# A new order of all engines for a two-block kernel (polynomial-sketch attention, then an MLP), with the products of VectorE and GpSimd kept apart

## The chip, the cores and the metric

The kernel runs on one core of one Trainium2 chip. The metric is the time of one execution in device microseconds (us). The engines are named as in the profile: PE is TensorE, PEld its weight loads, DVE VectorE, ACT ScalarE, POOL GpSimd, SP SyncE.

## The reference

All inputs are float32 except where the kernel decodes 64-bit words (the sketch matrices S1 and S2 and the two MLP weights are handed over as raw 64-bit floats and turned into float32 on the chip).

```python
# attention: batch 4, heads H=4, S=1088 tokens, D=32, r=8
def phi(x):                      # 64 features per token and head
    a = einsum('rd,bhsd->bhsr', S1, x); b = einsum('rd,bhsd->bhsr', S2, x)
    return einsum('bhsi,bhsj->bhsij', a, b).reshape(..., r*r)
q_p, k_p = phi(q), phi(k)
kv  = einsum('bhsf,bhsd->bhfd', k_p, v);  z = sum(k_p, axis=2)
num = einsum('bhsf,bhfd->bhsd', q_p, kv)
den = einsum('bhsf,bhf->bhs', q_p, z)[..., None] + 1e-06
x = (num / den) as (B, S, H*D)             # rows of 128
# MLP block, 128 -> 512 -> 128
xn = (x - mean) / sqrt(var + 1e-06) * g_ln
out = x + maximum(xn @ w_ch1, 0) @ w_ch2
```

## The kernel before, in words

The kernel is one long list of small operations, written as a string, `PROGRAM`, of 518 entries. Each entry names a Python function, which issues one to a few dozen instructions, and gives its arguments: the engine (V = DVE, A = ACT, G = POOL, S = the SP queue), the batch b or chunk c, the range u0 to u1 of the nine token groups of a batch, and banks of PSUM. No scheduler reorders anything afterwards: each engine executes its own entries in the order of the list, and waits only where data or a buffer demands it. An engine that has nothing to wait for therefore runs ahead of the place at which its entry stands in the list.

For each batch b the work goes like this. `turn_g`, `turn_r` transpose q and k (DVE, lines 414 and 424). `k_dir` or `k_feat`, `q_dir` or `q_feat` project them (PE, lines 448, 466, 554 and 587), and `k_cp`, `k_tok`, `q_cp`, `q_tok` bring the projections back to SBUF as `kf` and `fq`. `k_prod` forms the 64 products per token and head, `kp` (line 87, `times`), except that `k_prod0` does it from PSUM; `k_val` multiplies them with v (PE, line 519), and `k_vcp`, `k_spr`, `k_rcp` lay the result out as `kvr`. On the side of q, `q_ac` (product), `q_den` (sum), `q_rec` (reciprocal), `q_a2` (product) make the divided features, `q_prod` the 64 products, `qp`, and `q_turn` transposes these to `qpT` (DVE, line 634). `num b` (PE, line 648) then makes the rows of the attention; `num_cp` copies them to `xT` for the MLP, and `row_turn`, `row_wr`, `row_rd` bring the same rows, by way of DRAM, into `x` for the mean, variance and residual.

The MLP goes by chunks c of four groups of 128 rows (two chunks a batch; chunks 8 and 9 hold the ninth groups). `hid` is the first layer (PE, line 757), `relu` its activation (ACT or DVE), `sec` the second layer (PE, line 773). `st_bn`, `st_ag`, `st_pow` make 1/sqrt(var) (the power on POOL, line 743); `fin` (DVE) or `fin_a` with `fin_g` (ACT, then DVE or POOL, line 801) scale and add the residual, and `store` writes the result.

Before batch 0 the weights are decoded: `w_ex`, `w_bits`, `w_exf`, `w_mant`, `w_low`, `w_e2`, `w_e3`, `w_add`, `w_mul` (w = 0 for S1 and S2, 1 and 2 for the MLP's weights). `w_e3` (line 310) and `w_add` (line 315) have two operands in SBUF, as has `times`. `c_cg` and `fold` work the mean and the gain into the first weight. `fill` (line 247) is a product of ones with ones into a bank that nobody reads.

```python
    def times(eng, o, a, b):
        by[eng].tensor_tensor(out=o, in0=a, in1=b, op=ALU.mult)
    ...
    for line in PROGRAM.split(";"):
        if line.split():
            name, *args = line.split()
            ops[name](*(int(a) if a.isdigit() else a for a in args))
```

## Time and profile before

| | us |
|---|---|
| time, median of 3 runs (lowest, highest) | 107.59 (107.14, 107.84) |
| time of the profiled execution | 107.5 |
| its span in the profile | 105.6 |
| PE busy | 98.7 (93%) |
| DVE busy | 84.4 (80%) |
| POOL busy | 49.4 (47%) |
| ACT busy | 37.3 (35%) |

The span is what the trace covers; about 1.9 us of the profiled execution's time lie around it. The granted clock of TensorE was 1.0 throughout. PE's busy time contains 13.3 us of `fill`. In a timeline, a row gives start and length of a piece, the engine, the line, what it writes and reads, the shape and how often; a note in brackets tells how long the engine was idle before it and who ended that.

### The profile page before, as it was taken

To read this page: it belongs to the slowest core of one execution; us is meant where nothing else is said; L and a number is where in the kernel's file an instruction comes from. 1 tells how busy PE (TensorE), PEld (TensorE's weight loads), DVE (VectorE), ACT (ScalarE), POOL (GpSimd) and SP (SyncE) were. 2 spreads that over 40 slices of the span, in tenths; PEclk is the share of its full clock that TensorE was granted. 3 is DMA by queue.
4 is the path that set the end of the run, shared out by engine and by line. 5 is a ranking of instruction groups with operands and counts; after the bars stand their busy time and mean duration, and the time that the engine had idled before them with its cause. 6 is when DMAs were issued, how large, how long until landed. Compare 5 with 4: busy or idle time off the path is not lost.

```text
span 105.6 us, 3155 instructions
## 1 busy us (share of the span) xinstructions
PE 98.7 (93%) x1276; PEld 69.7 (66%) x1276; DVE 84.4 (80%) x243; ACT 37.3 (35%) x91; POOL 49.4 (47%) x65
## 2 busy tenths in 40 slices
...
GB/s 72 295 261 238 221 395 271 18 9 57 221 286 292 335 263 110 0 6 112 156 238 10 6 6 6 167 70 262 112 0 6 8 210 286 8 99 105 99 75 50
DMA packets 12639, 14.37 MB, mean 136 GB/s; under 512 B 2128, under 2 KB 9296, under 8 KB 12624
## 3 DMA queue, kind: packets, MB, share of 16 engines
...
q14 instruction: 5, 0.04, 0.1%
...
## 4 chain that ended last, share of the span: by engine, by line
PE 68%; DVE 23%; issue 2%; POOL 2%; ACT 0%; DVEq 0%
PE ALL L757 26%; PE ALL L773 25%; PE ALL L648 5%; DVE qp L87 5%; PE ALL L247 5%; DVE qpT L634 3%; PE ALL L519 2%; PE ALL L587 2%; DVE kp L87 2%; DVE kf L475 1%; DVE fq L596 1%; DVE bits L310 1%; POOL ex L305 1%; DVE kT L414 1%; DVE st L730 1%
## 5 line engine op out<-in xcount | busy, mean ns | idle before, releaser
L773 PEld LDWEIGHTS ALL<-w,hT 128*128 128x128 f32 x272 | 32.3, 192 | 5.5 <-issue 3.1
L773 PE MATMUL ALL<-w,hT 128*128 128x128 f32 x272 | 33.8, 278 | 0.0
L757 PE MATMUL ALL<-xT,w 128*128 128x512 f32 (+1 forms) x72 | 30.3, 550 | 0.0
L765 ACT ACTIVATE hT<-ALL 128x512 f32<-128x512 f32 (+2 forms) x34 | 16.6, 518 | 23.5 <-PE ALL L757 23.1
L743 POOL TENSOR_TENSOR rstd<-va,mhalf 128x4 f32<-128x4 f32 (+1 forms) x10 | 9.7, 972 | 24.1 <-DVE va L737 21.7
L757 PEld LDWEIGHTS ALL<-xT,w 128*128 128x128 f32 x72 | 12.5, 191 | 7.3 <-issue 5.5
L87 POOL TENSOR_TENSOR kp<-kf 128x1280 f32<-128x1280 f32 (+2 forms) x7 | 14.6, 2089 | 3.5 <-DVE kf L475 3.5
L247 PE MATMUL ALL<-ones 128*128 128x256 f32 (+1 forms) x28 | 13.3, 594 | 1.4 <-DVE m L195 1.4
L634 DVE STREAM_TRANSPOSE qpT<-qp 128x1280 f32<-128x1280 f32 (+2 forms) x9 | 11.0, 1230 | 0.1
L87 DVE TENSOR_TENSOR qp<-a,fq 128x512 f32<-128x512 f32 (+2 forms) x6 | 9.8, 1640 | 0.0
L87 POOL TENSOR_TENSOR qp<-a,fq 128x512 f32<-128x512 f32 (+3 forms) x4 | 8.6, 2142 | 1.6 <-DVE a L87 1.4
L767 DVE TENSOR_SCALAR hT<-ALL 128x512 f32<-128x512 f32 (+2 forms) x10 | 4.9, 498 | 5.2 <-PE ALL L757 5.2
L648 PE MATMUL ALL<-qpT,kvr 32*32 32x288 f32 (+2 forms) x320 | 7.2, 364 | 1.7 <-ACT ob L791 1.3
L791 ACT ACTIVATE ob<-ALL,rstd 128x128 f32<-128x128 f32 x20 | 6.6, 376 | 6.3 <-POOL rstd L743 4.5
L82 ACT COPY xT<-ALL 128x256 f32<-128x256 f32 x10 | 6.2, 639 | 6.3 <-DVE xh L710 3.3
L247 PEld LDWEIGHTS ALL<-ones 128*128 128x128 f32 x28 | 5.5, 220 | 4.3 <-issue 2.5
L710 DVE STREAM_TRANSPOSE xh<-ALL 128x256 f32<-128x256 f32 x16 | 6.6, 425 | 1.2 <-PE ALL L648 1.0
L648 PEld LDWEIGHTS ALL<-qpT,kvr 32*32 32x32 f32 x320 | 4.1, 103 | 4.5 <-ACT ob L791 1.5
L786 DVE SCALAR_TENSOR_TENSOR ob<-ALL,rstd,x 128x128 f32<-128x128 f32 x12 | 4.0, 349 | 3.8 <-PE ALL L773 2.5
L730 DVE BATCH_NORM_STATS2 st<-x 128x6 f32<-128x128 f32 x32 | 6.7, 274 | 0.0
L596 DVE STREAM_TRANSPOSE fq<-ALL 128x576 f32<-128x576 f32 x6 | 4.4, 765 | 1.8 <-PE ALL L587 1.8
L519 PEld LDWEIGHTS ALL<-kp,vn 128*32 128x32 f32 x288 | 4.2, 110 | 1.4 <-issue 0.9
(113 smaller groups left out, 114.8 us busy)
## 6 DMA issues: line engine op xcount, KB each, us to landing
...
xd<-xh SPq DMA_DIRECT2D x8, 256.0 KB, 2.1
x<-xd SPq DMA_DIRECT2D x8, 256.0 KB, 3.5
out_dram<-ob SPq DMA_DIRECT2D x7, 256.0 KB, 2.4
...
w_raw<-in_moe_w_ch_dram SPq DMA_DIRECT2D x2, 256.0 KB, 5.0
```

The costliest lines, as they stand in the source:

```text
L87: by[eng].tensor_tensor(out=o, in0=a, in1=b, op=ALU.mult)
L247: pe.matmul(bank(z, 0, w), ones[:, 0:P], ones[:, 0:w], start=True, stop=True)
L519: pe.matmul(bank(z, 0, F)[D * h : D * h + D], vn[b][:, TW * h + D * u : TW * h + D * (u + 1)], kp[:, H * F * u + F * h : H * F * u + F * ( ...
L634: dve.transpose(_ap(qpT, 0, P, 32 * u0, [[32, u1 - u0], [TW, 8], [1, 32]]), qp[:, H * F * u0 : H * F * u1])
L648: pe.matmul(bank(z[r], o, o + w)[D * h : D * h + D], kvr[b % 2][rows, DM * f + D * h : DM * f + D * h + D], qpT[rows, c : c + w], start=(f ...
L710: dve.transpose(_ap(xh[slot(c)], 0, P, 64 * n * i, [[32 * n, 2], [32, n], [1, 32]]), pair(z, P * (c % 2), [[32, n], [1, 32]]))
L730: dve.bn_stats(out=sts[slot(c)][:, 6 * t : 6 * t + 6], in_=row_ap(c, t))
L743: pool.tensor_tensor(out=rstds[slot(c)][:, 0:n], in0=vas[slot(c)][:, 0:n], in1=mhalf[:, 0:n], op=ALU.pow)
L757: pe.matmul(bank(z, 0, n), w1[:, P * j : P * (j + 1)], cols(c)[:, a : a + n], start=True, stop=True)
L765: act.activation(o, i, AF.Relu)
L773: pe.matmul(bank(z, DM * t, DM * (t + 1)), h[:, 512 * j + P * t : 512 * j + P * (t + 1)], w2[:, DM * j : DM * (j + 1)], start=(j == 0), st ...
L791: act.activation(ob(c)[:, P * t : P * (t + 1)], bank(z, P * t, P * (t + 1)), AF.Copy, scale=rstds[slot(c)][:, t : t + 1])
```

## The change

Only the list is changed; every function is as before. The 518 entries become 517: one `fill` of 512 columns is left out. All others stay, in another order on all engines, with other banks of PSUM, and some on another engine. Those that change engine are:

- `w_exf 1 256 512`, `w_mant 1 256 512` from DVE to ACT; `w_mant 2`, `w_add 2` to DVE (from ACT and POOL); `w_e2 2` from DVE to POOL
- `k_cp` of groups 0 to 3 of batch 0, and `k_vcp 2`, from ACT to DVE; `k_rcp 3` and `row_cp 8` from DVE to ACT; two stores change queue between SP and ACT
- `q_ac 1` (swapped halves), `q_ac 2` to DVE and `q_ac 3` to POOL; `q_a2` of `1 0 4`, `2 0 4` and `3 4 9` from DVE to POOL
- `q_prod 2 4 9` and `q_prod 3 0 4` from DVE to POOL
- `fin_g 0` and `fin_g 1` from DVE to POOL; four copies `num_cp` net from DVE to ACT, four `relu` net from ACT to DVE

Two lines of the diff stand for the rest:

```diff
-    w_e3 V 1 0 256; q_cp A 0 4 7 0 24; fill 1 512 4; fill 1 256 7; q_cp A 4 9 3 0 24;
-    q_ac V 0 0 4; c_cg G; sk_8 6; q_den 0 0 4; w_mul G 1 0 256; ld S q 1 0 34; q_rec 0 0 4;
+    k_prod0 3 6 5 3; w_add G 1 256 512; q_ac V 0 0 4; q_den 0 0 4; q_rec 0 0 4; ld_v S 1 1;
+    q_a2 V 0 0 4; k_prod G 0 6 9; fill 1 256 5; k_val 0 0 3 4; sk_8 6; q_ac V 0 4 9; c_rest;
```

DVE, the middle of batch 0 before. `kp` is `k_prod0` (one operand in PSUM), the L315 and L310 rows are `w_add` and `w_e3` of the first weight, `ac`, `den`, `rden`, `a` the steps `q_ac` to `q_a2`:

```order
L424 STREAM_TRANSPOSE qT_97<-qt 128x2x32
L296 TENSOR_SCALAR mant_115<-bits_112 128x256
L87 TENSOR_TENSOR kp<-ALL,kf_130 128x768
L315 TENSOR_TENSOR mant_115<-mant_115,low_116 128x256
L310 SCALAR_TENSOR_TENSOR bits_112<-w_raw,ex_113 128x256
L87 TENSOR_TENSOR ac_99<-fq 128x16x8
L394 TENSOR_TENSOR sk_128<-ALL,m_84 128x32
```

The same place now, from the decode to `q_ac`:

```order
L296 TENSOR_SCALAR mant_115<-bits_112 128x256
L315 TENSOR_TENSOR mant_115<-mant_115,low_116 128x256
L84 COPY kf_130<-ALL 128x192
L380 TENSOR_TENSOR skd_105<-ALL,m_85 128x4x16
L310 SCALAR_TENSOR_TENSOR bits_112<-w_raw,ex_113 128x256 x2
L414 STREAM_TRANSPOSE qT_97<-qt 128x2x8x32
L498 TENSOR_TENSOR zT<-ALL,m_83 128x32
L414 STREAM_TRANSPOSE qT_97<-qt 128x2x8x32
L424 STREAM_TRANSPOSE qT_97<-qt 128x2x32
L87 TENSOR_TENSOR kp<-ALL,kf_130 128x768 x2
L87 TENSOR_TENSOR ac_99<-fq 128x16x8
```

Both `w_e3` now stand in a row ahead of the transposes of q, and nothing of the weights' decode is left between these and `q_ac`.

POOL, from the second half of the first weight to the products of q of batch 0, before (`w1g` is `w_mul 1`, L347 is `c_cg`, `qp` is `q_prod`, `a` is `q_a2`):

```order
L87 TENSOR_TENSOR w1g<-mant_115,bits_112 128x256
L347 TENSOR_SCALAR cg_126<-ident_81,g_raw_67 128x128
L87 TENSOR_TENSOR w1g<-mant_115,bits_112 128x256
L231 MEMSET vn_74 64x4x32
L405 COPY skq_103<-skq_102 128x16
L87 TENSOR_TENSOR qp<-a_144,fq 128x512
L87 TENSOR_TENSOR a_144<-fq,rden_142 128x160
L87 TENSOR_TENSOR qp<-a_144,fq 128x768
```

Now, from `k_prod 0 6 9` on:

```order
L87 TENSOR_TENSOR kp<-kf_130 128x768
L239 MEMSET mhalf 128x4
L240 MEMSET eps 128x4
L242 MEMSET skq_101 128x8
L242 MEMSET skq_102 128x8
L242 MEMSET skq_103 128x8
L242 MEMSET skq_104 128x8
L87 TENSOR_TENSOR w1g<-mant_115,bits_112 128x256
L235 MEMSET ac_100 128x36
L347 TENSOR_SCALAR cg_126<-ident_81,g_raw_67 128x128
L87 TENSOR_TENSOR qp<-a_144,fq 128x512
L87 TENSOR_TENSOR a_144<-fq,rden_142 128x160
```

The first half of `w_mul 1` has moved ahead of `k_prod`, the second half behind it, and `c_cg` stands right before the first `q_prod`.

POOL, batch 2, before (L743 is `st_pow`; the first `qp` row is `q_prod 2 0 4`):

```order
L87 TENSOR_TENSOR ac_99<-fq 128x20x8
L87 TENSOR_TENSOR ac_99<-fq 128x16x8
L87 TENSOR_TENSOR kp<-kf_131 128x1024
L405 COPY skq_104<-skq_102 128x16
L87 TENSOR_TENSOR qp<-a_144,fq 128x1024
L743 TENSOR_TENSOR rstd_180<-va_177,mhalf 128x4
L87 TENSOR_TENSOR kp<-kf_131 128x1280
```

Now:

```order
L801 TENSOR_TENSOR ob_185<-ob_185,x_152 128x512
L87 TENSOR_TENSOR kp<-kf_131 128x1280
L87 TENSOR_TENSOR a_144<-fq,rden_142 128x128
L87 TENSOR_TENSOR qp<-a_144,fq 128x1024
L743 TENSOR_TENSOR rstd_180<-va_177,mhalf 128x4
L87 TENSOR_TENSOR qp<-a_144,fq 128x1280
L87 TENSOR_TENSOR kp<-kf_131 128x1024
```

Both products of q of batch 2 are now on POOL, one behind the other, with the power of chunk 2 between them.

Of the kernel before, what the change touches and what calls it, by code (L numbers as in the profile page):

```python
# [25 lines left out]
def kernel(  # L26
# [798 lines left out]
    ld S k 0 0 16; c_ones; ld_s A 1; c_iota; c_small; c_vpad 0; fill 1 512 7; c_masks; ld_s S 0;  # L825
    w_bits V 0 0 64; w_mant V 0 0 64; w_ex V 0 0 64; w_exf V 0 0 64; c_pads 0; w_e2 V 0 0 64;
    ld S k 0 16 34; w_addlow V 0 0 64; turn_g k 0 0 2; w_e3 V 0 0 64; fill 1 512 6; fill 1 512 7;
    ld_w S 1 2 4; s_heads V; c_ac 1; turn_r k 0; ld_w S 1 0 2; turn_g k 0 2 4; ld S q 0 0 34;
    ld_v S 0 0; w_low A 1 256 512; c_ident; sk 6; sk_0 6; c_ac 0; w_ex V 1 256 512; fill 1 256 7;
    k_dir 0 0 3 5; w_bits V 1 256 512; k_dir 0 3 6 7; sk_2 6; ld_g; k_cp A 0 3 6 7;  # L830
    w_exf V 1 256 512; k_dir 0 6 9 4; k_cp A 0 0 3 5; w_low A 1 0 256; ld_v S 0 1;
    w_ex V 1 0 256; w_mant V 1 256 512; sk_d 6; fill 1 512 3; w_e2 G 1 256 512; k_cp A 0 6 9 4;
    k_sum 0 4; ld_v S 0 2; fill 1 256 3; w_exf A 1 0 256; c_vpad 2; ld_vr S 0 0;
    w_bits V 1 0 256; w_e3 V 1 256 512; k_prod0 3 6 7 3; turn_g q 0 0 2; ld_v S 0 3; c_pads 1;
    ld_vr S 0 1; w_add G 1 256 512; sk_q 6; k_zs 0 4; k_sc 0 4; fill 1 256 3; k_prod G 0 6 9;
# [6 lines left out]
    fold_cp A 4 256 512; c_vpad 1; fill 1 256 7; q_den 0 4 9; ld_v S 1 2; k_vcp A 0 5; sk_qq 2;
    fold 3 0 256; k_spr 0 5; fold_cp A 3 0 256; fill 1 512 7; q_turn 0 2; q_prod G 0 2 4;
    q_rec 0 4 9; q_a2 G 0 4 9; k_rcp A 0 5; q_prod G 0 6 9; turn_g k 1 0 4; c_rest;
    q_prod V 0 4 6; w_low A 2 0 512; q_turn 2 4; turn_r k 1; k_feat 1 4 5; q_turn 4 9;
    num 0 0 4 6 7 2 3; num_cp A 0 0 0 4 6 7; ld_v S 1 3; w_ex V 2 0 512; k_tok 1 4 5;
    w_bits V 2 0 512; num 0 4 9 0 1 4 5; row_turn 0 1 2 3; row_turn 0 0 6 7;
    num_cp A 0 1 0 4 2 3; num_r V 0 0 1; k_sum 1 6; hid 7 0 3 2 4; num_cp V 0 0 4 8 0 1;
    w_exf A 2 0 512; hid 3 0 3 0 2; turn_r k 2; row_wr S 0; k_zs 1 6; k_sc 1 6; ld_v S 2 0;
    relu V 7 0 3 2 4; hid 2 0 1 2 4; num_cp A 0 1 4 8 4 5; row_turn 1 0 0 1; w_mant A 2 0 512;  # L850
    k_prod G 1 0 5; ld_v S 3 3; ld_v S 2 1; hid 1 0 1 0 2; hid 0 0 2 0 2; w_add G 2 0 512;
    w_e2 V 2 0 512; row_turn 1 1 4 5; relu A 2 0 1 2 4; row_rd S 0; relu A 1 0 1 0 2;
    hid 2 0 0 2 4; relu A 2 0 0 2 4; turn_r q 1; ld_vr S 1 0; turn_g q 1 0 4; ld_v S 1 0;
    hid 1 0 2 2 4; hid 5 0 0 0 2; relu A 1 0 2 2 4; relu A 3 0 3 0 2; row_wr S 1;
    relu A 5 0 0 0 2; w_e3 V 2 0 512; ld_vr S 2 0; hid 2 1 2 0 4; k_sccp V 1 6; q_feat 1 5 6 3 4;
    ld_v S 1 1; turn_g k 2 0 4; w_mul G 2 0 512; relu A 0 0 2 0 2; ld S q 3 0 34; st_bn 0;
    k_prod G 1 5 9; k_feat 2 0 1; sec 7 0 3; ld_vr S 1 1; q_tok 1 0 5 6; hid 6 1 1 0 4;
    q_tok 1 1 3 4; sec 4 0 2; hid 3 1 0 0 4; st_ag 0; q_ac V 1 4 9; c_vpad 3; q_den 1 4 9;
    sec 5 0 0; k_tok 2 0 1; k_val 1 0 9 1; row_rd S 1; k_sum 2 0; ld S k 3 0 34; ld S q 2 0 34;
    q_rec 1 4 9; q_ac G 1 0 4; st_pow 0; q_den 1 0 4; q_rec 1 0 4; q_a2 G 1 4 9;  # L860
    relu A 2 1 2 0 4; hid 2 1 3 0 4; k_vcp A 1 1; k_spr 1 1; relu A 6 1 1 0 4; q_a2 V 1 0 4;
    q_prod V 1 0 4; q_turn 0 4; q_prod G 1 4 9; k_zs 2 0; relu A 3 1 0 0 4; st_bn 1; sec 6 0 1;
    st_ag 1; fin_a 5 0 0; q_turn 4 9; fin_a 7 0 3; ld_v S 3 0; ld_v S 3 2; relu A 2 1 3 0 4;
    sec 7 1 1; k_sc 2 0; k_sccp V 2 0; sec 2 1 0; k_rcp A 1 1; turn_r k 3; fin_a 4 0 2; st_pow 1;
    turn_r q 2; ld_v S 2 2; turn_g k 3 0 4; turn_g q 2 0 4; fin_a 6 0 1; k_prod G 2 0 5;
    fin_a 7 1 1; fin_a 2 1 0; num 1 0 9 5 6 3 4; ld_v S 2 3; num_cp A 1 0 4 8 5 6;
    row_turn 3 0 5 6; row_turn 2 0 5 6; num_cp A 1 1 4 8 3 4; k_feat 3 1 2; k_tok 3 1 2;
    sec 7 1 2; num_cp A 1 0 0 4 5 6; num_r A 1 3 4; sec 0 1 3; k_prod G 2 5 9; q_feat 2 5 6 1 2;
    ld_vr S 2 1; fin_a 0 1 3; ld_v S 3 1; k_val 2 0 9 0; row_turn 3 1 3 4; row_wr S 3;
    fin_a 7 1 2; k_sum 3 7; ld_vr S 3 1; q_tok 2 0 5 6; row_turn 2 1 3 4; fin_g V 0;  # L870
    hid 6 8 3 0 1; q_tok 2 1 1 2; k_vcp A 2 0; hid 5 3 1 0 4; num_cp A 1 1 0 4 3 4;
    hid 4 2 2 0 4; q_ac G 2 4 9; k_spr 2 0; hid 2 2 0 0 4; relu V 2 2 0 0 4; q_ac G 2 0 4;
    hid 1 2 1 0 4; q_den 2 0 4; k_prod G 3 5 9; relu A 4 2 2 0 4; k_zs 3 7; q_rec 2 0 4;
    hid 4 2 3 0 4; k_sc 3 7; row_pe 8 2; q_den 2 4 9; k_rcp A 2 0; q_rec 2 4 9; relu A 4 2 3 0 4;
    row_wr S 2; q_a2 V 2 4 9; k_sccp V 3 7; sk_qq 3; c_act; q_a2 V 2 0 4; hid 0 3 0 0 4;
    relu A 1 2 1 0 4; hid 4 3 3 0 4; sec 1 2 0; row_rd S 3; row_rd S 2; sec 7 2 3;
    q_prod V 2 4 9; turn_r q 3; row_cp V 8 2; st_bn 2; q_prod G 2 0 4; hid 2 8 2 0 1; st_bn 8;
    relu A 0 3 0 0 4; relu A 2 8 2 0 1; st_ag 2; q_turn 0 4; st_pow 2; k_prod G 3 0 5;
    relu A 5 3 1 0 4; sec 0 2 2; sec 2 2 1; fin_a 7 2 3; hid 7 8 0 0 1; relu A 4 3 3 0 4;
    q_turn 4 9; turn_g q 3 0 4; hid 5 8 1 0 1; st_bn 3; fin_a 2 2 1; fin_a 0 2 2; fin_a 1 2 0;  # L880
    relu A 7 8 0 0 1; hid 4 3 2 0 4; relu A 4 3 2 0 4; store S 0 0 4; num 2 0 9 0 1 2 3;
    row_turn 5 0 0 1; ld_vr S 3 0; k_val 3 0 9 4; num_cp A 2 0 4 8 0 1; sec 7 3 3; st_ag 3;
    k_vcp A 3 4; st_ag 8; relu V 5 8 1 0 1; row_turn 4 1 2 3; relu A 6 8 3 0 1;
    num_cp V 2 0 0 4 0 1; st_pow 3; fin_a 7 3 3; fin_g G 2; row_turn 4 0 0 1;
    num_cp V 2 1 4 8 2 3; num_r A 2 0 1; row_turn 5 1 2 3; sec 6 3 0; fin_a 6 3 0; sec 5 3 1;
    num_cp A 2 1 0 4 2 3; q_feat 3 6 7 0 1; fin_g V 1; sec 2 3 2; row_wr S 4; st_pow 8;
    q_tok 3 0 6 7; fin_a 5 3 1; sec 5 8 0; k_spr 3 4; hid 7 5 0 0 4; hid 6 4 3 0 4;
    hid 3 4 0 0 4; q_tok 3 1 0 1; hid 1 5 3 0 4; hid 0 4 2 0 4; k_rcp V 3 4; q_ac V 3 0 4;
    q_den 3 0 4; q_ac V 3 4 9; row_wr S 5; relu A 6 4 3 0 4; hid 6 4 1 0 4; q_rec 3 0 4;
    relu A 7 5 0 0 4; relu A 1 5 3 0 4; hid 1 5 2 0 4; relu A 3 4 0 0 4; q_den 3 4 9;  # L890
    relu A 0 4 2 0 4; q_a2 G 3 0 4; relu A 6 4 1 0 4; sec 6 4 1; hid 0 5 1 0 4; q_rec 3 4 9;
    q_a2 V 3 4 9; q_prod V 3 0 4; fin 5 8 0; fin_a 2 3 2; q_turn 0 4; q_prod V 3 4 9; q_turn 4 9;
    row_rd S 5; relu A 1 5 2 0 4; relu A 0 5 1 0 4; row_rd S 4; store S 1 0 4; st_bn 5;
    sec 1 4 3; st_bn 4; st_ag 4; fin_g G 3; st_pow 4; fin_a 6 4 1; sec 0 4 2; fin_a 0 4 2;
    st_ag 5; store_r S 8 0; num 3 0 9 2 3 4 5; row_turn 7 0 2 3; num_r V 3 4 5; sec 7 5 2;
    row_turn 7 1 4 5; num_cp V 3 0 0 4 2 3; row_turn 6 0 2 3; store S 2 0 4;
    num_cp V 3 0 4 8 2 3; num_cp A 3 1 0 4 4 5; sec 0 4 0; fin_a 0 4 0; row_turn 6 1 4 5;
    row_wr S 6; num_cp V 3 1 4 8 4 5; sec 6 5 0; sec 3 5 1; row_wr S 7; st_pow 5; sec 5 5 3;
    hid 4 9 0 0 1; fin 6 5 0; hid 6 9 1 0 1; hid 2 6 3 0 4; fin 3 5 1; fin 7 5 2;
    relu V 2 6 3 0 4; hid 7 7 0 0 4; row_rd S 6; hid 3 9 3 0 1; hid 2 6 1 0 4; relu V 2 6 1 0 4;  # L900
    st_bn 6; row_rd S 7; store S 3 0 4; hid 0 6 2 0 4; relu V 0 6 2 0 4; fin_a 1 4 3;
# [43 lines left out]
```

165 lines of the change are left out of this document (82 added, 83 removed).

## The prediction

> **What bounds the kernel now.** I read the page first, then the timeline of PE for its gaps, then the timelines of DVE and POOL side by side. From the page, the shares (busy us, share of the span, instructions) and the chain that ended last:
>
> ```profile
> span 105.6 us, 3155 instructions
> PE 98.7 (93%) x1276; PEld 69.7 (66%) x1276; DVE 84.4 (80%) x243; ACT 37.3 (35%) x91; POOL 49.4 (47%) x65
> PE 68%; DVE 23%; issue 2%; POOL 2%; ACT 0%; DVEq 0%
> ```
>
> PE sets most of the end, DVE a quarter. The timeline of PE (start, length, what; in brackets the idle time before it) shows where each does:
>
> ```profile
> 20.46 1.02 PE L247 MATMUL ALL<-ones 128*128 128x512 f32 x2
> 21.41 1.05 PE L466 MATMUL ALL<-kT,sk 64*32 64x288 f32 x16
> 22.40 1.41 PE L648 MATMUL ALL<-qpT,kvr 32*32 32x128 f32 x80
> 24.18 1.04 PE L648 MATMUL ALL<-qpT,kvr 32*32 32x160 f32 x48 [0.37 <-DVE kf L475]
> 25.17 0.38 PE L490 MATMUL ALL<-kf 128*32 128x32 f32 x18
> 25.52 1.13 PE L757 MATMUL ALL<-xT,w 128*128 128x256 f32 x4
> 31.00 0.77 PE L466 MATMUL ALL<-kT,sk 64*32 64x288 f32 x16
> 43.19 1.59 PE L648 MATMUL ALL<-qpT,kvr 32*32 32x288 f32 x64 [1.33 <-ACT ob L791]
> 61.42 1.60 PE L648 MATMUL ALL<-qpT,kvr 32*32 32x288 f32 x64
> 69.78 6.17 PE L757 MATMUL ALL<-xT,w 128*128 128x512 f32 x14
> 75.78 1.15 PE L773 MATMUL ALL<-w,hT 128*128 128x128 f32 x8
> 79.57 1.60 PE L648 MATMUL ALL<-qpT,kvr 32*32 32x288 f32 x64
> 95.38 6.56 PE L773 MATMUL ALL<-w,hT 128*128 128x128 f32 x56
> ```
>
> The four L648 pieces are `num 0` to `num 3`. From 43.19 on PE has no gap: what lies behind `num 1` is its own work, 58.8 us to the last `sec` at 101.95. Ahead of it stand two waits, 0.37 and 1.33 us, and a head of 22 us in which PE is padded with `fill`. So a new order can win three things: a shorter head, the wait before `num 1`, and little else.
>
> The head belongs to DVE, and there the rows show products that stretch. Most rows here are pairs, one of POOL and the one of DVE that meets it; the first and the last met none:
>
> ```profile
> 10.18 0.43 DVE L310 SCALAR_TENSOR_TENSOR bits<-w_raw,ex 128x256 uint32<-128x256 uint32 x1 [0.57 <-POOL ex L305]
> 14.10 0.78 POOL L87 TENSOR_TENSOR w1g<-mant,bits 128x256 f32<-128x256 f32 x1
> 14.20 0.95 DVE L310 SCALAR_TENSOR_TENSOR bits<-w_raw,ex 128x256 uint32<-128x256 uint32 x1
> 16.52 0.68 DVE L87 TENSOR_TENSOR qp<-a,fq 128x512 f32<-128x512 f32 x1
> 18.92 1.51 POOL L87 TENSOR_TENSOR qp<-a,fq 128x768 f32<-128x768 f32 x1
> 19.27 1.71 DVE L87 TENSOR_TENSOR qp<-a,fq 128x512 f32<-128x512 f32 x1
> 35.52 2.42 POOL L87 TENSOR_TENSOR qp<-a,fq 128x1280 f32<-128x1280 f32 x1
> 35.72 3.30 DVE L87 TENSOR_TENSOR qp<-a,fq 128x1024 f32<-128x1024 f32 x1
> 54.96 1.48 DVE L87 TENSOR_TENSOR qp<-a,fq 128x1280 f32<-128x1280 f32 x1
> 55.12 3.13 POOL L87 TENSOR_TENSOR qp<-a,fq 128x1024 f32<-128x1024 f32 x1 [1.42 <-DVE a L87]
> 72.14 1.22 DVE L87 TENSOR_TENSOR qp<-a,fq 128x1024 f32<-128x1024 f32 x1
> ```
>
> One form takes 0.68 us at 16.52 and 1.71 at 19.27. In the second case POOL's product ends at 18.92 + 1.51 = 20.43, and DVE's ends 0.55 later. At 35.72 the same: POOL ends at 37.94, DVE 1.08 later, where 1.22 is the whole cost alone. At 54.96 DVE was first, and POOL ends 3.13 - 1.32 = 1.81 after it. So two such products don't share; the later one waits for the whole earlier one.
>
> **The head, step by step.** DVE's last step ahead of `num 0` is the third `q_turn`, and the next instruction starts at 23.05:
>
> ```profile
> 7.78 0.23 DVE L373 TENSOR_TENSOR sk<-ALL,m 128x64 f32<-128x64 f32 x1 [1.26 <-PE ALL L369]
> 8.53 0.28 DVE L287 TENSOR_SCALAR exf<-ex 128x256 f32<-128x256 uint32 x1
> 8.91 1.23 POOL L305 TENSOR_SCALAR ex<-exf 128x256 uint32<-128x256 f32 x1 [5.60 <-DVE exf L287]
> 12.83 0.25 DVE L296 TENSOR_SCALAR mant<-bits 128x256 f32<-128x256 uint32 x1
> 12.95 1.07 POOL L305 TENSOR_SCALAR ex<-exf 128x256 uint32<-128x256 f32 x1
> 14.86 0.65 POOL L347 TENSOR_SCALAR cg<-ident,g_raw 128x128 f32<-128x128 f32 x1
> 15.07 0.28 DVE L87 TENSOR_TENSOR ac<-fq 128x128 f32<-128x128 f32 x1
> 23.05 0.38 DVE L274 TENSOR_SCALAR ex<-w_raw 128x512 uint32<-128x512 uint32 x1
> ```
>
> Gone: the two meetings, 0.95 - 0.43 = 0.52 and 1.71 - 0.68 = 1.03; `w_exf` and `w_mant`, 0.28 and 0.25 long, to ACT, which is free there; since DVE's instructions overlap by some 0.08 they free 0.4. Added: the `k_cp` of 128x192 on DVE, taken as 0.3; `turn_r k`, moved behind the wait at 7.78, as 0.2 (both are estimates, sized like the small rows here). The mask operations that start DVE's program now stand behind the small decode, in the idle 1.26 us before 7.78: nothing; without that cover they would cost up to 1.3. New: both `w_e3` in a row wait for two `w_e2` of POOL back to back. These run from 8.9 to 8.9 + 1.23 + 1.07 = 11.2, and DVE gets there at about 10.55: 0.65 of waiting, where it now waits 0.57. Sum: -0.52 - 1.03 - 0.4 + 0.3 + 0.2 + 0.1 = -1.35, so `q_turn` would end at 21.7.
>
> But the list doesn't hold POOL back. Its rows in the new order need data only. From 11.2 on come `w_mul` 0.78, `w_add` of the same size, `k_prod` 1.51 (as `qp` of that size) and small memsets, about 0.6: the second `w_mul` comes at about 14.9, and DVE comes to `q_ac` (15.07, less 0.3) at 14.8. `c_cg` ends at 14.9 + 0.78 + 0.65 = 16.3, and DVE's first `q_prod` comes at 16.52 - 0.3. Who is first is decided by a tenth of a us. If POOL wins both, DVE waits some 0.7 and 1.0: +1.7. I take half of it: DVE ends 0.5 earlier.
>
> PE has its own floor. The missing `fill` is worth 0.95 (20.46 to 21.41); `k_feat`, which took 1.0 until 22.40 and 0.77 at 31.00, may lose 0.25 more of hidden wait, and 0.37 goes because `num 0` now uses other banks than `k_tok`. That lets the first `hid` start at most 1.6 earlier than 25.52. On DVE's side, `hid` needs the end of `q_turn` plus `k_tok` (0.77, the form of L596 below), `w_ex` (0.38) and a `num_cp` (an estimate of 0.5), 1.6 us, against 2.5 now (23.05 to 25.52). That is 0.5 + 0.9 = 1.4 earlier, or 0.55 with all meetings against it. **Term 1: -1.2**, just under both, bounds -1.6 and -0.4.
>
> **Batch 1.** The wait of 1.33 before `num 1` ends with ACT's row by its label, but `q_turn` of batch 1 ends at that time too:
>
> ```profile
> 41.54 1.50 DVE L634 STREAM_TRANSPOSE qpT<-qp 128x1280 f32<-128x1280 f32 x1
> ```
>
> Before it DVE lost 3.30 - 1.22 = 2.08 at 35.72. The new order keeps these same two products, one on each engine, with both `q_a2` ahead of them on POOL. One must still wait for the other; but DVE now stands waiting when the second `q_a2` ends, and if it goes first, the first `q_turn` runs beside POOL's product. Against that, `w_mant`, `w_add` and a `relu` come onto DVE here. Counted from the new start, `num 1` is ready between 41.3 and 42.6, and PE, with one `sec` more done ahead of it, comes there at about 41.5. **Term 2: -0.7**, bounds -1.33 and 0.
>
> **Batches 2 and 3.** PE's content stays. What is new is that both products of q of batch 2 are POOL's, with a power between. From the end of `q_feat 2`, DVE's steps to `q_rec` take some 2.6 us (two `q_tok` of 0.77, and four small rows like `ac`); then `q_a2`, `q_prod` of 1024 (1.94 by the 2.42 of 1280), the power (1.02) and `q_prod` (2.42), and 1.50 for `q_turn`. Two waits add to it: the one behind `k_prod`, and `st_bn 2`, which now stands on DVE ahead of the second `q_den` and waits for its rows to return from DRAM:
>
> ```profile
> xd<-xh SPq DMA_DIRECT2D x8, 256.0 KB, 2.1
> x<-xd SPq DMA_DIRECT2D x8, 256.0 KB, 3.5
> L743 POOL TENSOR_TENSOR rstd<-va,mhalf 128x4 f32<-128x4 f32 x8 | 8.1, 1020 | 22.1 <-DVE va L737 19.7 <-DVE mv L736 2.3
> L596 DVE STREAM_TRANSPOSE fq<-ALL 128x576 f32<-128x576 f32 x6 | 4.4, 765 | 1.8 <-PE ALL L587 1.8
> ```
>
> By these, with `row_turn` done some 4 us after the start of `num 1`, `st_bn 2` starts at about 10.2 (4.0 + 2.1 + 3.5 and two issues), its power ends at 13.7, `q_prod` at 16.1, `q_turn` at 17.5. PE comes to `num 2` after 18.2, as it does now (43.19 to 61.42; seven `hid` of 0.86 between, from 69.78 to 75.78 in seven). So 0.7 us of cover; behind it each us late is a us of the span. For batch 3 the same count gives 16.5 against 17.3. **Term 3: 0**, bounds -0.5 and +3.
>
> The end keeps its form: last `sec`, one `fin`, a store of half a chunk, now on ACT's queue. 0.
>
> **The sum:** -1.2 - 0.7 = -1.9, so a span of 103.7. The profiled execution has 107.5 for 105.6; 105.6 is its new time, and the median of the runs lies 0.1 above it: **105.7 us**.
>
> The Trainium skill, SBUF — State Buffer, section Who interferes with whom, says that a DVE instruction with two SBUF inputs contends with any GpSimd instruction that reads SBUF, so with POOL's TENSOR_SCALAR as well. The row of `ac` at 15.07 does not show it: its 0.28 us lie inside `c_cg`, 14.86 to 15.51.
>
> **Rivals.**
>
> Products still meet. POOL runs ahead, wins the races of the head, and term 1 is -0.4; the two products of batch 1 go in the old order, and term 2 is 0. For it: nothing in the list binds POOL. Against: only 3 or 4 places are left. 107.6 - 0.4 = 107.2 us.
>
> Slower: **POOL's queue in batches 2 and 3.** `st_bn 2` holds the second `q_den` on DVE, and `q_prod 2 4 9` stands behind the power of the same chunk. If the rows come back later than the two landings say, `num 2` is late by all that exceeds 0.7 us, and `num 3`, which has `st_bn 4` ahead of `q_den`, likewise. With 2.5 us more on each, 2 x 1.8 = +3.6, less the gains of 1.9, gives 109.3; the point where the gain is eaten is 0.95 us a batch beyond the cover. For it: the reads meet v's and q's loads. Against: PE's gaps are nil there now with similar round trips.
>
> More: both waits go, DVE wins the races, and 0.5 is left over behind `num 1`: -1.6 - 1.3 - 0.5 = -3.4, so 104.2 us. Against: every condition has to hold.
>
> POOL's TENSOR_SCALAR locks out DVE's products as well. Then `w_add 1` waits for the first `w_e2` (0.8 of its 1.23), and the 512 wide `w_add 2` for the third, about 1.0, which delays `num 1`: 105.7 + 1.8 = 107.5 us. Against: the row of `ac`. The page named above states this rule.
>
> **Chances.** Forecast (104.6 to 106.5) 0.44; products still meet 0.18; POOL's queue 0.24; more 0.10; the wider lock 0.04. A measurement here tells about 1% from no change, 106.5 and 108.7. Faster: the forecast, "more", and a little of the second: 0.56. Same: the rest of the second and the fourth, and the weak half of POOL's queue: 0.20. Slower: 0.24 less those, and what nobody foresaw: 0.24. The range, with 0.2 left out: 104.1 to 109.0; the likeliest's own is 104.6 to 106.5.
>
> **What would show it.** Right: in the new timeline the first `hid` near 24.3, `num 1` near 41.5 with a gap under 0.6, no DVE `qp` row of 1.7 or 3.3, PE without gaps from there on. Wrong: a gap of PE over 1 us before `num 2` or `num 3`, with POOL's `qp` or DVE's `st` before it; a `w_e3` or `ac` row on DVE of 0.9 beside a POOL product; a first `hid` at 25 or later.

## The result, and the profile after

The change takes **106.98 us** in the median of 20 runs (106.49 to 107.72); the kernel before took 107.69 beside it (20 runs). The ratio is 0.9935, 95% interval 0.9912 to 0.9959: 0.7 us faster, inside the 1% that I had called "same". Forecast were 105.7 and a gain of 1.9.

The page of the profiled execution of the change, its span and shares, the clock in 40 slices of 2.65 us, and the chain that ended last:

```profile
span 106.0 us, 3145 instructions
PE 98.9 (93%) x1274; PEld 70.0 (66%) x1274; DVE 78.1 (74%) x235; ACT 38.5 (36%) x92; POOL 58.2 (55%) x72
PEclk9999859999999999999999999999999999999997
PE 77%; DVE 8%; DMA 8%; SPq 2%; issue 1%; ACT 1%; DVEq 0%
```

DVE is busy 78.1 us, not 84.4. PE is busy 98.9, as before, but in this execution that contains a dip of the clock (the 8 and the 5 of the clock line) that the page of before did not have. The places on PE's timeline (L504 is `k_sc`, L554 `q_dir`, L648 `num`, the first L757 the first `hid`):

```profile
12.44 0.43 PE L504 MATMUL ALL<-zT,s2b 128*128 128x32 f32 x2 [1.39 <-DVE zT L498]
13.68 3.31 PE L554 MATMUL ALL<-skd,qT 128*128 128x96 f32 x18
26.70 1.62 PE L757 MATMUL ALL<-xT,w 128*128 128x256 f32 x6
44.03 1.60 PE L648 MATMUL ALL<-qpT,kvr 32*32 32x288 f32 x64
62.92 1.60 PE L648 MATMUL ALL<-qpT,kvr 32*32 32x288 f32 x64
80.67 1.60 PE L648 MATMUL ALL<-qpT,kvr 32*32 32x288 f32 x64
95.59 6.57 PE L773 MATMUL ALL<-w,hT 128*128 128x128 f32 x56
```

This execution is the slowest of the 20 of the change (107.72 us) and the only one with a mean granted clock under 0.99 (0.979; the others have 0.992 to 1.0). A second execution of the change, experiment 8 below, has no dip, and PE is busy 97.3 there. The same places in it, with the first sketch on DVE (L373) ahead:

```profile
7.16 0.18 DVE L373 TENSOR_TENSOR sk<-ALL,m 128x64 f32<-128x64 f32 x1
12.12 0.41 PE L504 MATMUL ALL<-zT,s2b 128*128 128x32 f32 x2 [1.25 <-DVE zT L498]
12.88 2.18 PE L554 MATMUL ALL<-skd,qT 128*128 128x96 f32 x18
25.49 1.63 PE L757 MATMUL ALL<-xT,w 128*128 128x256 f32 x6
43.08 1.60 PE L648 MATMUL ALL<-qpT,kvr 32*32 32x288 f32 x64
94.58 6.57 PE L773 MATMUL ALL<-w,hT 128*128 128x128 f32 x56
```

and in a second trace of the kernel before:

```profile
7.97 0.22 DVE L373 TENSOR_TENSOR sk<-ALL,m 128x64 f32<-128x64 f32 x1 [1.64 <-PE ALL L369]
25.69 1.13 PE L757 MATMUL ALL<-xT,w 128*128 128x256 f32 x4
43.35 1.59 PE L648 MATMUL ALL<-qpT,kvr 32*32 32x288 f32 x64 [1.32 <-ACT ob L791]
95.55 6.56 PE L773 MATMUL ALL<-w,hT 128*128 128x128 f32 x56
```

The four traces, cut at the starts of these rows and at the end of the last:

| us | start to L373 | to first `hid` | to `num 1` | to the end of the last `sec` | rest | span |
|---|---|---|---|---|---|---|
| before | 7.78 | 17.74 | 17.67 | 58.75 | 3.66 | 105.6 |
| before, again | 7.97 | 17.72 | 17.66 | 58.76 | 3.69 | 105.8 |
| change | 7.28 | 19.42 | 17.33 | 58.13 | 3.84 | 106.0 |
| change, again | 7.16 | 18.33 | 17.59 | 58.07 | 3.75 | 104.9 |

So the head behind the first sketch got **longer**, by 0.6 (1.7 where the clock dipped), and what lies between the first `hid` and the last `sec` got shorter by 0.76 (0.96 in the first trace). Counted from the start of the span, the first `hid` of the second trace (25.49) comes where before had it (25.52 and 25.69). The first column is not settled by these four; it comes back under "What stays open".

### The profile page after: what moved, and what is told of

It reads as the page before. It is cut to its first block, busy times and chain, and to the rows that moved or that the text cites. A ratio compares the mean times of both kernels' runs of the same rounds, so it can differ in the third digit from the quotient of the medians.

```text
span 106.0 us, 3145 instructions
## 1 busy us (share of the span) xinstructions
PE 98.9 (93%) x1274; PEld 70.0 (66%) x1274; DVE 78.1 (74%) x235; ACT 38.5 (36%) x92; POOL 58.2 (55%) x72
## 4 chain that ended last, share of the span: by engine, by line
PE 77%; DVE 8%; DMA 8%; SPq 2%; issue 1%; ACT 1%; DVEq 0%
PE ALL L773 30%; PE ALL L757 29%; DMA qt<-in_q_dram 8%; PE ALL L648 5%; PE ALL L519 3%; PE ALL L554 3%; DVE qpT L634 3%; PE ALL L587 2%; PE ALL L466 1%; DVE qp L87 1%; DVE ac L87 1%; DVE kT L414 1%; PE ALL L247 1%; PE ALL L490 1%; SPq L158 1%; PE ALL L504 1%
## 5 line engine op out<-in xcount | busy, mean ns | idle before, releaser
L773 PE MATMUL ALL<-w,hT 128*128 128x128 f32 x272 | 33.1, 277 | 0.0
L757 PE MATMUL ALL<-xT,w 128*128 128x512 f32 (+1 forms) x72 | 30.7, 556 | 0.0
L765 ACT ACTIVATE hT<-ALL 128x512 f32<-128x512 f32 (+2 forms) x30 | 14.8, 515 | 18.4 <-PE ALL L757 15.2
L743 POOL TENSOR_TENSOR rstd<-va,mhalf 128x4 f32<-128x4 f32 (+1 forms) x10 | 9.5, 956 | 20.0 <-DVE va L737 17.2
L757 PEld LDWEIGHTS ALL<-xT,w 128*128 128x128 f32 x72 | 12.1, 190 | 9.6 <-issue 5.6
L87 POOL TENSOR_TENSOR kp<-kf 128x1024 f32<-128x1024 f32 (+2 forms) x7 | 14.5, 2086 | 3.7 <-DVE kf L475 3.2
L247 PE MATMUL ALL<-ones 128*128 128x256 f32 (+1 forms) x26 | 12.2, 596 | 1.4 <-DVE ones L190 1.4
L87 POOL TENSOR_TENSOR qp<-a,fq 128x1280 f32<-128x1280 f32 (+3 forms) x6 | 12.1, 2021 | 2.2 <-DVE sk L394 1.9
L767 DVE TENSOR_SCALAR hT<-ALL 128x512 f32<-128x512 f32 (+2 forms) x14 | 7.2, 521 | 4.4 <-PE ALL L773 3.3
L82 ACT COPY xT<-ALL 128x256 f32<-128x256 f32 x14 | 8.1, 651 | 5.4 <-PE ALL L648 2.7
L648 PE MATMUL ALL<-qpT,kvr 32*32 32x288 f32 (+2 forms) x320 | 7.1, 364 | 0.4 <-DVE kf L475 0.4
L305 POOL TENSOR_SCALAR ex<-exf 128x256 uint32<-128x256 f32 (+1 forms) x3 | 4.1, 1377 | 5.4 <-ACT exf L285 5.2
L801 POOL TENSOR_TENSOR ob<-ob,x 128x512 f32<-128x512 f32 x4 | 6.0, 1492 | 0.0
L648 PEld LDWEIGHTS ALL<-qpT,kvr 32*32 32x32 f32 x320 | 3.9, 103 | 3.0 <-DVE qpT L634 0.8
```

What stands on the lines that cost most here:

```text
L82: act.copy(o, i)
L247: pe.matmul(bank(z, 0, w), ones[:, 0:P], ones[:, 0:w], start=True, stop=True)
L648: pe.matmul(bank(z[r], o, o + w)[D * h : D * h + D], kvr[b % 2][rows, DM * f + D * h : DM * f + D * h + D], qpT[rows, c : c + w], start=(f ...
L743: pool.tensor_tensor(out=rstds[slot(c)][:, 0:n], in0=vas[slot(c)][:, 0:n], in1=mhalf[:, 0:n], op=ALU.pow)
L757: pe.matmul(bank(z, 0, n), w1[:, P * j : P * (j + 1)], cols(c)[:, a : a + n], start=True, stop=True)
L765: act.activation(o, i, AF.Relu)
```

## Where the head lost it: products still meet

DVE and POOL in the second trace of the change, each row of DVE with the row of POOL that it met:

```profile
14.49 0.88 DVE L87 TENSOR_TENSOR ac<-fq 128x128 f32<-128x128 f32 x1
14.49 0.72 POOL L87 TENSOR_TENSOR w1g<-mant,bits 128x256 f32<-128x256 f32 x1
16.63 1.56 DVE L87 TENSOR_TENSOR qp<-a,fq 128x512 f32<-128x512 f32 x1
16.53 1.11 POOL L87 TENSOR_TENSOR qp<-a,fq 128x512 f32<-128x512 f32 x1 [0.90 <-DVE sk L394]
21.09 0.65 DVE L87 TENSOR_TENSOR qp<-a,fq 128x512 f32<-128x512 f32 x1
21.84 1.51 DVE L634 STREAM_TRANSPOSE qpT<-qp 128x1280 f32<-128x1280 f32 x1
```

`q_ac` takes 0.88 and not 0.28, the first `q_prod` 1.56 and not 0.68: 0.60 + 0.88 = 1.48 us. The two meetings of before are gone (its `qp` of 1.71 is 0.65 at 21.09), and two others have come in their place. POOL comes first at 16.53 by the order of the list: it had been idle for 0.90 us until DVE's `q_a2` and `sk_8` were done, and DVE then had a second `q_ac` to do before its own `q_prod`. In the first trace, where DVE came to the first `q_ac` 1.6 us later, POOL's `qp` met the second `q_ac` instead:

```profile
17.61 1.19 DVE L87 TENSOR_TENSOR ac<-fq 128x160 f32<-128x160 f32 x1
17.55 1.07 POOL L87 TENSOR_TENSOR qp<-a,fq 128x512 f32<-128x512 f32 x1 [1.93 <-DVE sk L394]
```

## The experiments

All stand beside runs of the kernel before, whose medians were 107.56 to 107.64.

**1 to 3: PE's idle time before `k_sc`.** In the change PE stands 1.25 to 1.39 us idle there. The first run puts a `fill` of 512 columns into that place (before has one of 256 there), the second moves `k_zs` and `k_sc` ahead of the transposes of q, the third does both.

```diff
-    k_cp A 0 3 6 5; turn_g q 0 0 2; k_cp A 0 6 9 4; k_sum 0 2; k_zs 0 2; turn_g q 0 2 4; k_sc 0 2;
+    k_cp A 0 3 6 5; turn_g q 0 0 2; k_cp A 0 6 9 4; k_sum 0 2; fill 1 512 3; k_zs 0 2; turn_g q 0 2 4; k_sc 0 2;   # 1
+    k_cp A 0 3 6 5; k_cp A 0 6 9 4; k_sum 0 2; k_zs 0 2; k_sc 0 2; turn_g q 0 0 2; turn_g q 0 2 4;                # 2
+    k_cp A 0 3 6 5; k_cp A 0 6 9 4; k_sum 0 2; k_zs 0 2; k_sc 0 2; fill 1 512 3; turn_g q 0 0 2; turn_g q 0 2 4;  # 3
```

> The change, with one more product of ones (512 columns, 0.86 us) between k_sum and k_zs of batch 0, where PE stood idle for 1.39 us. VectorE still reaches k_zs as late as before, so nothing but PE's clock can gain. Clock theory (the idle time lets the granted clock fall, and q_dir, 3.1 us instead of 2.0, is what that costs): q_dir back to 2.0 us, q_ac at about 15.1 instead of 16.1, a median of 106.2 to 106.5 against 106.98 of the change. Late-k_zs theory (the lateness of k_zs behind the transposes of q alone is the loss): no gain, 106.9 to 107.1. Race theory (q_ac of groups 4 to 8 loses 0.9 us behind GpSimd's q_prod): that row stays at about 1.2 us in either case.

> The change, with k_sum, k_zs and k_sc of batch 0 (and the copy that k_sum needs) moved ahead of the two transposes of q. PE no longer waits 1.39 us for k_zs, but it waits for the transposes ahead of q_dir instead, about 0.9 us, in two pieces. Late-k_zs theory: q_dir starts 0.8 us earlier, 106.2 to 106.5. Clock theory: PE is idle nearly as long in sum, so the clock still falls in some executions and q_dir stays between 2.0 and 3.1; 106.6 to 107.0. Race theory: the row of q_ac stays near 1.2 us, unless the start of q_prod on GpSimd moves with it.

> Both edits: k_sum, k_zs and k_sc ahead of the transposes, and the product of 512 columns behind them. If the clock and the late k_zs each cost their part, the two gains add: first hid at about 25.2 instead of 26.7, 105.6 to 106.1. If only the race matters, 106.8 to 107.0 with the row of q_ac unchanged.

Measured: 107.09 (ratio 0.9970, 0.9933 to 1.0007), 106.99 (0.9966, 0.9923 to 1.0009) and 106.87 (0.9948, 0.9908 to 0.9989): all as the change. Rows of the first run, PE and then DVE:

```profile
13.11 0.41 PE L504 MATMUL ALL<-zT,s2b 128*128 128x32 f32 x2 [0.26 <-DVE zT L498]
15.47 0.88 DVE L87 TENSOR_TENSOR ac<-fq 128x128 f32<-128x128 f32 x1
17.62 1.56 DVE L87 TENSOR_TENSOR qp<-a,fq 128x512 f32<-128x512 f32 x1
```

PE's idle time is 0.26, and the two stretched rows are as in the second trace of the change. The expected row of 1.2 for the second `q_ac` did not come (0.31 or 0.32 in all three): POOL holds the first `q_prod` instead. From L373 to the first `hid` the three traces have 18.46, 18.47 and 18.46, the change 18.33. So PE's idle time there costs nothing of itself, and the clock, 1.0 in these three traces, is no cause of the median.

**4: the head of before with the rest of the change.** The list of before up to `num 0`, with the banks that the rest wants, then the change's entries.

```diff
-    k_feat 1 4 5; q_turn 4 9; num 0 0 4 6 7 2 3; num_cp A 0 0 0 4 6 7; ...   # before
+    k_feat 1 2 3; q_turn 4 9; ... k_tok 1 2 3; ... num 0 0 4 0 1 4 5;        # then as in the change
```

> The head of the kernel before (all entries ahead of num 0, with k_feat 1 on banks 2 and 3), and from num 0 on the order of the change. Theory that the change loses in the head what it wins behind it: num 0 starts at 22.4 as before, the wait before num 1 (1.33 us) is gone, 106.0 to 106.5. Rival, that the rest is no better than before (the gain at num 1 is given back in batches 2 and 3, or comes from the one more sec ahead of num 1 alone): 107.3 to 107.7.

Measured: 106.43 (105.78 to 106.98), ratio 0.9907 (0.9872 to 0.9943). L373 to the first `hid` is 17.48, from there to `num 1` 17.45. Before has 17.7 for the first, with the same entries up to the last `q_turn`; so 0.25 of this stage comes with the order from there on. That order alone gains 1.15 in the median, and the new head gives some 0.5 of it back. The kernel still has the meeting of before:

```profile
18.73 1.71 DVE L87 TENSOR_TENSOR qp<-a,fq 128x512 f32<-128x512 f32 x1
```

**5: the meetings of the change undone.** The second experiment, with `w_mul` of the second half, `k_prod` and `q_ac` of the second groups moved so that DVE goes first, or POOL is done; the small memsets moved out of POOL's way.

```diff
-    k_prod0 3 6 5 3; w_add G 1 256 512; q_ac V 0 0 4; ... q_a2 V 0 0 4; k_prod G 0 6 9; ... sk_8 6; q_ac V 0 4 9;
-    q_prod V 0 0 2; ... w_mul G 1 256 512;
+    k_prod0 3 6 5 3; w_add G 1 256 512; w_mul G 1 256 512; k_prod G 0 6 9; q_ac V 0 0 4; ... q_ac V 0 4 9; q_a2 V 0 0 4;
+    q_prod V 0 0 2; sk_8 6;
```

> The order of e2_zs, with the meetings of the head taken apart by order alone: GpSimd's small memsets moved ahead of its decode, the second half of w_mul 1 ahead of k_prod, and on VectorE q_ac of groups 4 to 8 ahead of q_a2, and q_prod of groups 0 and 1 directly behind q_a2, so that VectorE reaches it before GpSimd reaches its own. Race theory (each us that VectorE wins ahead of q_ac is lost again to a product of GpSimd that came first: 0.6 us at q_ac, 0.9 at q_prod in e2_zs): the first q_prod back to 0.7 us, q_ac at most 0.6, first hid at about 25.0, a median of 105.7 to 106.2. Rival (PE's own content or the load of q bounds the head): 106.8 to 107.1.

Measured: 106.78 (106.31 to 107.28), ratio 0.9908 (0.9876 to 0.9941): 0.2 below the change, which is inside the noise, and not the 105.7 to 106.2 of the race theory. `q_ac` fell to 0.58 and `q_prod` to 0.69, but PE now waited (PE, then DVE):

```profile
17.46 0.70 PE L247 MATMUL ALL<-ones 128*128 128x256 f32 x2 [0.77 <-DVE sk L394]
23.25 0.78 DVE L475 STREAM_TRANSPOSE kf<-ALL 128x576 f32<-128x576 f32 x1 [0.69 <-PE ALL L466]
```

What a `fill` writes is read by nobody, but this one goes into a bank (6) from which `sk_8` (L394) has still to read, and `sk_8` stood behind `q_prod`. The 0.77 that PE lost there came out as 0.69 at `k_tok`. Experiment 10 takes this away.

**6: the head of before with one entry moved,** so that its `q_prod` comes when POOL's is nearly over.

```diff
-    q_prod V 0 4 6; w_low A 2 0 512; q_turn 2 4; turn_r k 1;
+    w_low A 2 0 512; q_turn 2 4; turn_r k 1; q_prod V 0 4 6;
```

> The kernel of e4_old_head with one entry moved: q_prod of groups 4 and 5 of batch 0 stands behind the q_turn of groups 2 and 3, so that it comes when GpSimd's product of groups 6 to 8 is nearly over (in e4_old_head it waits 1.0 us for it). Race theory: it costs 0.7 to 1.2 us instead of 1.7, q_turn ends 0.5 to 0.7 us earlier, 105.7 to 106.0 against 106.43. Rival, that PE bounds the head of that kernel: 106.3 to 106.5.

Measured: 106.10 (105.62 to 106.66), ratio 0.9851 (0.9805 to 0.9897). The row of 1.71 is now

```profile
19.66 0.99 DVE L87 TENSOR_TENSOR qp<-a,fq 128x512 f32<-128x512 f32 x1
```

and from `q_ac` to the end of the third `q_turn` it takes 7.55, not 8.04. But from L373 to the first `hid` it takes 17.45, as in experiment 4, for this execution lost as much ahead of `q_ac`, where the lists are the same. There POOL's `w_mul` met DVE's `w_add` (0.82, not 0.41), in experiment 4 it met `w_e3`:

```profile
13.64 0.82 DVE L315 TENSOR_TENSOR mant<-mant,low 128x256 f32<-128x256 f32 x1
13.46 0.73 POOL L87 TENSOR_TENSOR w1g<-mant,bits 128x256 f32<-128x256 f32 x1
```

The 0.33 between the two medians is thus not shown by the whole head, and their intervals overlap.

**7: who goes first in batch 1.** In the change DVE's `q_prod 1` starts 0.4 ahead of POOL's. Here it stands behind `st_bn 1`, so that POOL starts first.

```diff
-    q_a2 G 1 4 9; q_prod V 1 0 4; ... q_prod G 1 4 9; k_rcp A 1 3; st_bn 1; q_turn 0 4;
+    q_a2 G 1 4 9; ... q_prod G 1 4 9; k_rcp A 1 3; st_bn 1; q_prod V 1 0 4; q_turn 0 4;
```

> The change with q_prod V 1 0 4 moved behind st_bn 1 on VectorE, 0.8 us later, so that GpSimd's q_prod 1 4 9 comes first, as in the kernel before. If the gain at num 1 comes from VectorE going first: the row of 1.4 us becomes 2.5 or more, q_turn 4 9 ends about 1.2 us later, a wait of about 1 us stands again before num 1, 107.7 to 108.2. Rival, that it comes from the missing waits on banks alone: 106.9 to 107.2.

Measured: 108.52 (108.06 to 109.05), ratio 1.0092 (1.0062 to 1.0122), 1.5 slower than the change, and 0.3 more than the theory's 108.2. The change's second trace, DVE and POOL:

```profile
37.05 1.39 DVE L87 TENSOR_TENSOR qp<-a,fq 128x1024 f32<-128x1024 f32 x1
37.44 3.27 POOL L87 TENSOR_TENSOR qp<-a,fq 128x1280 f32<-128x1280 f32 x1
```

and this kernel, POOL, DVE and PE:

```profile
37.53 2.39 POOL L87 TENSOR_TENSOR qp<-a,fq 128x1280 f32<-128x1280 f32 x1
38.28 0.87 DVE L730 BATCH_NORM_STATS2 st<-x 128x6 f32<-128x128 f32 x4 [0.97 <-DMA x<-xd]
39.07 1.93 DVE L87 TENSOR_TENSOR qp<-a,fq 128x1024 f32<-128x1024 f32 x1
44.44 1.59 PE L648 MATMUL ALL<-qpT,kvr 32*32 32x288 f32 x64 [1.46 <-DVE qpT L634]
```

The wait before `num 1` is back, 1.46, and with it the time. `st_bn`'s own wait for its rows (0.97) is a part of it, so the 1.5 is not the meeting's price alone.

**8: the change again**, for the second trace above.

> The change itself once more, for a second profile and for its time on the same chip as the others. If the 1.39 us that PE is idle ahead of k_zs lowers the clock each time, q_dir takes about 3.1 us again; if that was one execution, q_dir takes 2.0 us, and q_ac loses about 0.6 us to w_mul on GpSimd instead. Time by either: 106.8 to 107.2.

Measured: 106.95 (106.62 to 107.55), ratio 0.9947 (0.9916 to 0.9979), clock 0.998 behind an idle 1.25 us.

**9: before again.**

> The kernel before once more, for a second trace of it. Its only trace has its first sketch operation (L394/L367 side) late, sk at 6.86, and a span of 105.6; from sk to the first hid 18.66, from there to num 1 17.67. If sk comes late there by chance: the new trace has sk between 5.7 and 6.5, the same 18.66 (within 0.3) behind it, and a span near 105.0. If the gain of 0.7 in the medians is a shorter head after all: from sk to the first hid it takes 19.3 or more here, and the change's 19.3 is no longer. Time 107.6, ratio 1.00.

Measured: 107.45 (107.06 to 108.15), ratio 0.9992 (0.9961 to 1.0022). Neither theory held: the first sketch is late again (7.97), and the head behind it has the same length as in the first trace (17.72).

**10 and 11: what bounds the head without meetings.** Experiment 5 with `sk_8` early, and then with the 512 wide `fill` behind POOL's first `q_prod` left out.

```diff
-    k_cp V 0 0 3 7; sk_d 6; w_e3 V 1 0 256; ... q_prod V 0 0 2; sk_8 6;
+    k_cp V 0 0 3 7; sk_d 6; sk_8 6; w_e3 V 1 0 256; ... q_prod V 0 0 2;      # 10
-    q_prod G 0 2 4; ld_vr S 1 0; fill 1 512 6; q_turn 0 2;
+    q_prod G 0 2 4; ld_vr S 1 0; q_turn 0 2;                                 # 11
```

> e5_races_undone with one entry moved: sk_8 from behind the first q_prod of DVE to directly behind sk_d, ahead of both w_e3. In e5 the bank that it empties held PE's last 512 wide fill back for 0.77, and k_tok waited 0.69 for k_feat. Theory (DVE's meetings gone, PE held by that bank): the gap of 0.77 goes, first hid 18.4 behind sk instead of 19.1, time 106.1 to 106.3. Rival (PE's content of fills, folds and k_feat is the bound in any case): first hid still 19.0 behind sk, time 106.8.

> The run before, less the fill of 512 columns behind q_prod of groups 2 and 3 in batch 0 (0.95 us of PE). If PE's content bounds the head: 0.5 to 0.95 faster than e10_sk8_early. If DVE's chain does: within 0.2 of it. If fewer fills lower the granted clock: slower than it, with a clock under 1.0 behind the missing fill.

Measured: 105.93 (105.46 to 106.28), ratio 0.9831 (0.9786 to 0.9877), and 106.15 (105.45 to 106.44), ratio 0.9847 (0.9797 to 0.9897). Experiment 10, DVE with the row of POOL at the first, then PE:

```profile
7.44 0.19 DVE L373 TENSOR_TENSOR sk<-ALL,m 128x64 f32<-128x64 f32 x1
14.84 0.58 DVE L87 TENSOR_TENSOR ac<-fq 128x128 f32<-128x128 f32 x1
13.77 1.50 POOL L87 TENSOR_TENSOR kp<-kf 128x768 f32<-128x768 f32 x1
16.61 0.69 DVE L87 TENSOR_TENSOR qp<-a,fq 128x512 f32<-128x512 f32 x1
20.95 1.51 DVE L634 STREAM_TRANSPOSE qpT<-qp 128x1280 f32<-128x1280 f32 x1
7.68 2.22 PE L448 MATMUL ALL<-sk,kT 128*128 128x64 f32 x18 [0.50 <-DVE sk L373]
24.68 1.62 PE L757 MATMUL ALL<-xT,w 128*128 128x256 f32 x6
42.02 1.60 PE L648 MATMUL ALL<-qpT,kvr 32*32 32x288 f32 x64
```

From L373 to the first `hid` it takes 17.24, 1.1 less than the change and 0.5 less than before. The 0.77 of PE and the 0.69 of DVE are gone. (The figures of 18.4 and 19.0 counted from PE's first sketch matmul. That starts at 5.70 here, so by that mark it is 18.98, the rival's figure; but DVE takes its result only at 7.44, with PE waiting 0.50 for it, so L373 is the better mark, chosen after the result. The time, 105.93, is below the theory's 106.1 to 106.3 and 0.9 from the rival's 106.8.) Without the `fill` the head takes 17.21, and the clock is 1.0 behind its place: DVE's chain bounds the head, not PE's content. Experiment 10 has the lowest median of this study, 1.0 us below the change and 1.6 below before; 11 and 6 are not clear of it.

## Why the prediction was wrong, step by step

**Term 1, the head, failed.** Forecast was the first `hid` 1.2 us earlier; it came 0.6 later, counted from the first sketch, with "a first `hid` at 25 or later" named as the sign of being wrong (26.70 and 25.49). Two steps of it were off, and a third in part:

- *"I take half of it."* The races between DVE and POOL were seen (+1.7 if POOL wins both), and half was taken because they are decided by a tenth of a us. They were as close as forecast: POOL's `w_mul` starts with `q_ac` to the hundredth, its `q_prod` 0.10 ahead of DVE's. But half is not what a race gives: POOL won both in the second trace and in experiments 1, 2 and 7 (0.88 or 0.89, and 1.56, each time), at a cost of 0.60 + 0.88 = 1.48, and it won the second in experiment 3 too (1.56). Ahead of the second POOL, which the prediction had busy with `c_cg` until 16.3, stood idle until DVE's `q_a2` was done. The order thus settles such a race as long as nothing else delays one side: where DVE waited for `fq` ahead of the first `q_ac`, it lost 0.37 there in experiment 3 and nothing in the first trace.
- *The sum of -1.35.* Even with the meetings taken away but for 0.3 of one (experiment 10), the first `hid` gains 0.5, not 1.2. DVE comes to `q_ac` 7.40 after L373, 7.29 in before, and not at 7.0 (14.8 less 7.78); from there the third `q_turn` ends after 7.62 us, where 21.7 less 14.8 was 6.9, and before has 8.04. The first part of the sum was 0.4 too good, of which 0.3 is DVE's wait for the two `w_e2` (0.65 in the sum, 0.96 here); the second was 0.7 too good, of which 0.3 is the `q_ac` of 0.58. The other 0.5 stays open. About 0.25 of the 0.5 that is won comes with the order behind the last `q_turn` (experiment 4). The floor put down to PE did not bind (experiment 11).
- *The mask operations, "nothing".* In the change's own two traces they cost under 0.1. But with them DVE is not ready for the first sketch before 7.16 (7.43 in experiments 5 and 10). In experiments 7 and 10 PE's matmul for it (L369) ends at 6.50 and 6.55, and DVE starts at 7.16 and 7.44: 0.6 to 0.9 us that the cover does not hide. With the head of before DVE waits for PE there in all four traces, 0.26 to 1.64 us.

The wait of DVE for the two `w_e2` is 0.42 and 0.43 in the two traces of the change, and 0.96 in all the other traces of the new head; 0.65 lies between.

**Term 2, batch 1, held.** PE has no gap before `num 1` in the change, no `qp` row of DVE's is 1.7 or 3.3 long there, and experiment 7 brings the gap back by turning the two around. **Term 3 held too.** The second trace of the change, DVE, POOL, DVE and PE in batch 2:

```profile
52.80 0.87 DVE L730 BATCH_NORM_STATS2 st<-x 128x6 f32<-128x128 f32 x4 [0.31 <-DMA x<-xd]
55.33 1.03 POOL L743 TENSOR_TENSOR rstd<-va,mhalf 128x4 f32<-128x4 f32 x1 [0.50 <-DVE va L737]
58.76 1.51 DVE L634 STREAM_TRANSPOSE qpT<-qp 128x1280 f32<-128x1280 f32 x1 [0.70 <-POOL qp L87]
61.92 1.60 PE L648 MATMUL ALL<-qpT,kvr 32*32 32x288 f32 x64
```

Counted from `num 1` (43.08), `st_bn 2` starts at 9.7 (forecast 10.2), the power ends at 13.3 (13.7), `q_turn` at 17.2 (17.5), and PE comes at 18.8 (18.2). The cover is 1.6 us and nothing of POOL's queue comes through. Terms 2 and 3 together were -0.7; first `hid` to last `sec` measures -0.76 and -0.96. Only 0.1 to 0.3 of it lies ahead of `num 1`, for PE does one `sec` more there (56 of its matmuls, not 48); the rest lies behind, where that `sec` is missing.

**The rivals.** "Products still meet" is what happened, in the head though not in batch 1: 107.2 forecast, 106.98 measured, with a chance of 0.18. It had the better mechanism for term 1, but that its time is so near is luck: it still had the head 0.4 shorter, where it came 0.6 longer, and it gave batch 1 nothing, where the stages behind the first `hid` won 0.76. "POOL's queue in batches 2 and 3" fell by the rows above. "POOL's TENSOR_SCALAR locks out DVE's products as well" fell too. The first trace of the change, DVE and POOL:

```profile
31.13 0.69 DVE L315 TENSOR_TENSOR mant<-mant,low 128x512 f32<-128x512 f32 x1
30.15 1.98 POOL L305 TENSOR_SCALAR ex<-exf 128x512 uint32<-128x512 f32 x1
```

The product of 512 columns lies wholly inside POOL's row and takes 0.69, as the `qp` of 512 that met nothing (0.68). The Trainium skill, SBUF — State Buffer, section Who interferes with whom, has a DVE instruction with two SBUF inputs contend with a GpSimd instruction that reads SBUF. Here DVE's products are held by GpSimd's products, and not by this TENSOR_SCALAR. Whether POOL's TENSOR_SCALAR waits for a DVE product is open: `c_cg` took 0.65 in before, where it started inside DVE's `w_e3` (14.20 to 15.15), and 0.36 in the first trace of the change, where it met no product of DVE. So the row of `ac`, inside that `c_cg`, was weak evidence.

**What stays open.** Behind the first sketch the second trace of the change is only 0.1 shorter than before (97.74 against 97.82), while the medians differ by 0.65 to 0.7. If these executions are typical behind it, the rest lies ahead of it. There L373 starts at 7.78 and 7.97 in the two traces of before, at 7.28 and 7.16 in the two of the change; but in experiments 1, 2, 3 and 11, whose edits all lie behind it, at 8.02, 7.64, 7.90 and 8.12, and with the head of before in experiments 4 and 6 at 7.25 and 6.96. What differs are PE's first fills, the same six matmuls in every kernel. Before and experiment 10:

```profile
1.44 5.49 PE L247 MATMUL ALL<-ones 128*128 128x512 f32 x6 [1.44 <-DVE m L195]
1.44 4.32 PE L247 MATMUL ALL<-ones 128*128 128x512 f32 x6 [1.44 <-DVE ones L190]
```

They take 5.49 us in five of the thirteen traces and between 4.28 and 5.39 in the others, with both heads. So that stage varies by over 1 us between executions, whichever the head; the mask operations of the new head only limit how early it can end. That the change starts earlier on the average was not shown, and where the rest of its 0.7 lies stays open. By what lies behind the first sketch, experiments 4 and 10 are 1.1 and 1.4 shorter than before, and by the medians 1.15 and 1.6; for these two the account closes nearly. In experiments 1, 2, 6 and 7 some 0.5 is open in the same way.
